# Routing of a mixture-of-experts kernel: some lists of tokens made at once, rows transposed within the first phase, counts over 128 columns

## The chip, the cores and the metric

The kernel runs as one program on one core of a Trainium2 chip. The metric is the device time of an execution in microseconds; the time of a kernel is the median of its runs.

## The reference

Three layers follow each other. First comes attention over 4 x 8 heads of 576 positions with a window of 32, plain or dilated by 4. Its output is a table `x` of N = 2304 tokens with DM = 512 features. The second layer gives each token to one of E = 8 experts, each with room for `cap` = 288, in the order of all 18,432 logits; the third gives each token to its two best experts. An expert is two matrices with a ReLU between them (512 x 1024 and 1024 x 512), all in float32.

```python
logits = x @ w_gate
order = np.argsort(-logits.flatten())
for idx in order:
    tok, e = (int(idx) // E, int(idx) % E)
    if assigned[tok] >= 0 or counts[e] >= cap:
        continue
    assigned[tok] = e
    counts[e] += 1
...
for e in range(E):
    mask = assigned == e
    h = np.maximum(x[mask] @ w1[e], 0.0)
    out[mask] = h @ w2[e]
```

The third layer takes this `out` as its `x`; change and prediction hardly touch it.

## The kernel before

Attention leaves the tokens transposed (features on partitions) in `x0T`. `rows` transposes them back, 128 tokens in four TensorE transposes (L434), copies them with ScalarE (L436) and stores them to the table `xr` in memory through SP's queue (L437). There are 18 such rows. From `xr` the tokens of an expert are gathered later.

`routing` finds the experts one after the other, in the order in which they fill up, since the reference's greedy rule can be computed so: among the tokens not yet given away, find the smallest logit at which some expert has 288 tokens. Logits are turned into integers of 20 bits, cut into digits of 6, 7 and 7 bits, and each digit is one *round*:

- VectorE compares all tokens with each value of the digit, the indicator `I` (L526): 64 values in the first round of an expert, 128 in the other two.
- TensorE counts per expert (L544): 18 matmuls, for 18 x 128 tokens, with `I` as the weights (64 or 128 columns) and 8 moving columns. The first of an expert's three counts is called the leading count here.
- VectorE marks the values at which an expert is full (`sat`, L546), a matmul sums the marks over partitions (L555), and VectorE narrows the remaining digits (`w`, L559).

After three rounds the expert is known (`ei`, L569), and so are its tokens. Two matmuls (L505, L506) number them, the prefix sums, and `choices` (from L477) prepares the next expert on VectorE. `lister` turns the numbers into a list: VectorE makes a matrix `R` (six instructions at L673), TensorE multiplies it with token numbers in 18 matmuls of 96 columns (L680), VectorE makes the indices (L682 to L685). Then POOL starts three gathers of 96 tokens from `xr` (L769), TensorE transposes them (L783), and the expert's feed-forward, FFN1, can run: 192 matmuls of 288 columns at L759 (float32 in three products of split halves), 96 up and 96 down. The weights of an expert are loaded through SP's queue (L702, L712) once `ei` is known, in eight pieces, and split by ScalarE (`whi`, L720) and VectorE (`wlo`, L724).

The order of instructions on every engine is written out by the program itself as it is built: a small plan holds a clock for TensorE (`pe`) and VectorE (`dv`), and the pieces of routing, of lists and of transposes are put between the matmuls of FFN1 where the plan takes their inputs to be ready. Engines run their instructions in that order. The list of expert 0 is made at once on VectorE and those of the others in pieces from the first round of the next expert on (`self.lister(k - 1, ...)`); their matmuls are set in later by `end`, as a task of their own. `ROWS0` says how many rows are transposed between the steps of routing, here 18 rows over the eleven steps of expert 0 and half of expert 1. An expert's transposes may be started when `ready[k]` has passed in the plan, 5 us behind the start of its gathers.

In the order that results, FFN1 of expert 0 has three rounds beside it (those of expert 2), the pause behind it one, FFN1 of expert 1 six (the last two of expert 3, three of expert 4, the first of expert 5) and FFN1 of expert 2 five: eleven beside experts 1 and 2, and none beside the later ones. Experts are numbered from 0 in the order in which they are found; the last one, 7, takes what is left and needs no rounds.

There is a second copy of the program, with other digits (`self.exact`), which runs only if the first finds that its 20 bits didn't separate the tokens.

Of the kernel before, what the change touches and what calls it, by code (L numbers as in the profile page):

```python
# [21 lines left out]
N, DM, E, F = 2304, 512, 8, 1024  # L22
CAP = N // E
NT = N // 128
# [20 lines left out]
SPLITS2F = (1.0, 4.0, 10.0, 16.0, 42.0, 44.0, 46.0, 48.0)  # L45
CUTS = ((0, 5), (5, 4))
LOAD = (3.0, 5.0)
ROWS0 = (4, 1, 2, 1, 2, 1, 2, 1, 2, 1, 1)
WARM = (14, 2, 9)
HOP = (0.13, 0.2)  # L50
SLACK = (0.1, 0.4, 0.0, 0.2)
# [94 lines left out]
class Body:  # L146
# [292 lines left out]
    def routing(self):  # L439

        nc, L, wk = self.nc, self.L, self.wk
# [22 lines left out]
        w0 = wk.tile([128, NT], BF, name="w0")  # L464
        wd = wk.tile([128, NT], F32, name="wd")
        I = self.hp.tile([128, 1 << max(DIGITS), NT], BF, name="I", tag="hl0")
        rk2 = wk.tile([128, 2, NT], F32, name="rk2")
        EQ2 = EQ.rearrange("p a c -> p (a c)")
        nc.gpsimd.memset(al, 1.0)
# [50 lines left out]
        for k in range(E - 1):  # L520
            ei = self.st.tile([1, 1], I32, name=f"ei{k}")
            self.EV[k] = ei

            for r in range(NR):
                nb = 1 << DIGITS[r]
                V.tensor_tensor(I[:, :nb], self.thr[:, :nb], w[:, None, :].to_broadcast([128, nb, NT]), op=OP.is_lt)  # L526
                if r == 0:
                    V.tensor_tensor(dg[:, 1:], u[:, 1:2, :].to_broadcast([128, NR - 1, NT]), self.shift[:, 1:],
                                    op=OP.logical_shift_right)
                    for b in sorted(set(DIGITS[1:])):  # L530
                        i = 1 + DIGITS[1:].index(b)
                        j = i + DIGITS[1:].count(b)
                        V.tensor_scalar(dg[:, i:j], dg[:, i:j], (1 << b) - 1, None, op0=OP.bitwise_and)
                    V.tensor_scalar(dd[:, 1:], dg[:, 1:], 1.0, None, op0=OP.add)
                    if k:
                        leftover()
                    if k > 1:
                        self.lister(k - 1, place(pk))
                self.chain((0.3 if r else 0.0) + nb * NT / 1920 + 0.06)
                self.shade(COUNT)  # L540
                yield "pe", k, COUNT
                pc = self.rt.tile([128, 512], F32, name="r")
                for c in range(NT):
                    nc.tensor.matmul(pc[:nb, :E], I[:, :nb, c], OH[:, c, :], start=c == 0, stop=c == NT - 1)  # L544
                sat = wk.tile([128, 1 + E], BF, name="sat")
                V.tensor_scalar(sat[:nb, 1:], pc[:nb, :E], float(CAP), None, op0=OP.is_ge, op1=OP.max,  # L546
                                accum_out=sat[:nb, 0:1])
                more = r + 1 < NR
                if more:
                    V.scalar_tensor_tensor(wd, w, 256.0, dd[:, r + 1, :], op0=OP.mult, op1=OP.add)  # L550
                self.chain(0.08)
                self.shade(0.15)
                yield "pe", k, 0.03
                pj = self.rt.tile([128, 512], F32, name="r")
                nc.tensor.matmul(pj[:, :1 + E], (self.c256 if more else self.ones)[:nb, :], sat[:nb],  # L555
                                 start=True, stop=True)
                if more:
                    w = wk.tile([128, NT], BF, name=f"w{1 + r % 2}")
                    V.tensor_scalar(w, wd, pj[:, 0:1], None, op0=OP.subtract)  # L559
            V.scalar_tensor_tensor(E8, pj[:, 1:1 + E], pj[:, 0:1], prio, op0=OP.is_equal, op1=OP.mult)  # L560
            V.tensor_scalar(G[:, 0], w, pj[:, 0:1], None, op0=OP.is_gt)
            V.tensor_reduce(es, E8, axis=AX.X, op=OP.max)
            V.tensor_scalar(G[:, 1], w, pj[:, 0:1], None, op0=OP.is_equal)
            V.scalar_tensor_tensor(EQ, pm[:, None, :].to_broadcast([128, 2, NT]), es, G,
                                   op0=OP.is_equal, op1=OP.mult)
            V.tensor_scalar(E8, E8, es, -BIG, op0=OP.is_equal, op1=OP.mult)
            scan()
            V.tensor_tensor(L, L, E8[:, None, :].to_broadcast(sh), op=OP.add)
            V.tensor_scalar(ei, es[0:1, :], -1.0, float(E), op0=OP.mult, op1=OP.add)  # L569
            self.chain(1.2)  # L570
            self.shade(0.15)
            yield "expert", k, 0.05
            pk = prefix()
            if k == 0:
                self.lister(0, place(pk))
                self.flush()
                self.chain(4.0)
            choices()
            self.chain(3.0)

            dA = wk.tile([128, NT], BF, name="dA")
            V.scalar_tensor_tensor(dA, EQ[:, 0], 0.5, dd[:, 0], op0=OP.is_lt, op1=OP.mult)
            V.scalar_tensor_tensor(tk, pk[:, NT:2 * NT], float(CAP), EQ[:, 1], op0=OP.is_lt, op1=OP.mult)
            V.scalar_tensor_tensor(al[:, 0], EQ[:, 0], 0.5, al[:, 0], op0=OP.is_lt, op1=OP.mult)
            V.scalar_tensor_tensor(w0, tk, 0.5, dA, op0=OP.is_lt, op1=OP.mult)
            V.scalar_tensor_tensor(al[:, 0], tk, 0.5, al[:, 0], op0=OP.is_lt, op1=OP.mult)
            w = w0

        k = E - 1
        leftover()  # L590
        self.lister(k - 1, place(pk))
        while self.low:
            t, f = self.low.pop(0)
            f()
# [49 lines left out]
            while q:  # L644
                q.pop(0)[1]()

    def lister(self, k, rk):

        nc, wk = self.nc, self.wk
        V = nc.vector  # L650
# [22 lines left out]
            V.tensor_tensor(R[:, c:c + 3], self.c("iota")[:, None, :GB].to_broadcast([128, 3, GB]),  # L673
                            rm[:, c:c + 3, None].to_broadcast([128, 3, GB]), op=OP.is_equal)

        def end():
            yield 0.0, max(0.0, self.dv + HOP[0] - self.pe)
            pl = self.rt.tile([128, 512], F32, name="r")
            for c in range(NT):
                nc.tensor.matmul(pl[:GB, :6], R[:, c, :], A6[:, c], start=c == 0, stop=c == NT - 1)  # L680
            cp6 = wk.tile([GB, 3, 2], F32, name="cp6")
            V.tensor_copy(cp6.rearrange("p a v -> p (a v)"), pl[:GB, :6])  # L682
            idx = self.st.tile([GB, 3], I32, name=f"idx{k}")
            V.scalar_tensor_tensor(idx, cp6[:, :, 0], 128.0, cp6[:, :, 1], op0=OP.mult, op1=OP.add)
            V.tensor_copy(self.tok[:GB, 3 * k:3 * k + 3, :], cp6)  # L685
            self.IDX[k] = idx
            self.listed(k)
            yield 0.85, 0.0

        self.low = [(0.45, begin), (0.3, middle)]  # L690
        self.low += [(0.37, lambda c=c: hot(c)) for c in range(0, NT, 3)]
        self.low += [(0.0, lambda: self.start(end()))]


# [381 lines left out]
    def build(self):  # L1076
# [26 lines left out]
        def gathers():  # L1103

            while lists and lists[0] <= nflip:
                k = lists.pop(0)
                self.gather1(k)
                ready[k] = self.pe + 5.0

        def listed(k):  # L1110
            lists.append(k)
# [107 lines left out]


        c = 0
        for n in ROWS0:
            step()
            self.rows(x0T, c, c + n, self.tr, "t", self.gp)
            c += n
# [231 lines left out]
```

## Time and profile before

| | us |
|---|---|
| median of 3 runs | 958.6 (957.18 to 958.78) |
| the profiled execution | 956.22 |
| its span (first to last instruction) | 954.3 |
| TensorE busy (matmuls) | 879.1 (92%) |
| VectorE busy | 516.8 (54%) |
| ScalarE busy | 368.0 (39%) |
| POOL busy | 185.6 (19%) |
| DMA, mean | 132 GB/s |

The span is cut into 40 slices of 24 us on the page. TensorE is at 9 tenths in most of them; the slices that are not lie between 96 and 216 us, where attention ends and the first experts run, and there the granted clock falls to 5 tenths in one slice and to 6 in another. Of the chain that ended last, 60% of the span are the feed-forward's matmuls (L759), 3% the counts (L544). To read: busy time is a sum over stages that are limited by different things; PEclk is the granted clock of TensorE, 1.00 for 2.4 GHz and 0.50 for 1.2 GHz; an instruction's idle time before it is put down to the wait that ended last.

### The profile page before, as it was taken

Reading aid. Unit: us, or ns where it says so; the run is one execution under the profiler, and the core shown is the slowest. Engines: PE = TensorE matmul, PEld = TensorE weight load, DVE = VectorE, ACT = ScalarE, POOL = GpSimd, SP = SyncE. Lnnn points to the kernel's source line nnn. Section 1 sums busy time; section 2 is a strip of 40 time slices with the busy share of each in tenths; the row PEclk is TensorE's granted clock in tenths of the full one; section 3 lists DMA queues with packets and bytes.
Section 4 is the critical chain, followed back from the end, with each engine's and each line's share of the span. In section 5 each row is a group of like instructions: output and inputs, shape, how many; then the busy total and the mean of one; then the engine's idle time right before and its main releaser. Section 6 shows DMA issues by size and latency. Waiting matters only on the chain.

```text
span 954.3 us, 16949 instructions
## 1 busy us (share of the span) xinstructions
PE 879.1 (92%) x6725; PEld 797.0 (84%) x6725; DVE 516.8 (54%) x1540; ACT 368.0 (39%) x669; POOL 185.6 (19%) x154
## 2 busy tenths in 40 slices
PE   8989849859999999989989999999999999999994
PEld 5777648748989999978978898989989898898983
DVE  6666546657878754396567552735436363372310
ACT  2557423323324464545523433334333333333310
POOL 4656010011112100001013122121222113122011
PEclk9899757968879999989999999999999999999998
DMA  9970452523444866536433554453544535433112
GB/s 306 273 186 2 155 172 75 175 87 101 132 151 148 271 227 197 166 111 191 138 98 81 152 145 88 134 143 75 161 78 140 122 89 155 92 119 77 23 23 36
DMA packets 59641, 126.33 MB, mean 132 GB/s; under 512 B 7456, under 2 KB 14880, under 8 KB 59552
## 3 DMA queue, kind: packets, MB, share of 16 engines
q1 hardware_dynamic: 46080, 94.53, 31.7%
q0 software_dynamic: 10496, 25.77, 14.0%
q10 hardware_dynamic: 2976, 4.85, 1.6%
q8 instruction: 55, 0.90, 0.4%
q14 instruction: 34, 0.28, 0.1%
HBM read 100.49 MB, written 24.72 MB: 131 GB/s over the span
## 4 chain that ended last, share of the span: by engine, by line
PE 76%; DVE 11%; DMA 5%; ACT 3%; issue 3%; POOL 1%; ACTq 0%; SPq 0%; POOLq 0%; DVEq 0%
PE m L759 60%; PE r L544 3%; DVE wlo L724 3%; PE s L246 2%; PE t L1033 2%; PE o L297 2%; DMA kt<-in_k_dram 1%; PE ps L278 1%; PE t L434 1%; DVE hl L747 1%; DMA g<-xr,idx 1%; PE t L783 1%; PE t L840 1%; PE t L821 1%; DVE I L526 1%
## 5 line engine op out<-in xcount | busy, mean ns | idle before, releaser
L759 PE MATMUL m<-xh,whi 128*128 128x384 f32 (+2 forms) x768 | 239.4, 312 | 3.3 <-DVE hl L747 3.3
L759 PE MATMUL m<-xh,wlo 128*128 128x384 f32 (+2 forms) x768 | 239.3, 312 | 0.5 <-DVE wlo L724 0.3
L759 PE MATMUL m<-xl,whi 128*128 128x384 f32 (+2 forms) x768 | 238.9, 311 | 0.0
L724 DVE TENSOR_TENSOR wlo<-raw,whi 128x512 fp32r<-128x512 f32 x256 | 163.2, 682 | 56.9 <-ACT whi L720 56.9
L747 DVE SCALAR_TENSOR_TENSOR hl<-m,hh 128x256 fp32r<-128x256 f32 (+2 forms) x192 | 89.6, 474 | 161.3 <-ACT hh L746 138.6
L746 ACT ACTIVATE hh<-m 128x256 fp32r<-128x256 f32 (+2 forms) x192 | 81.7, 427 | 193.7 <-PE m L759 179.3
L759 PEld LDWEIGHTS m<-xh,whi 128*128 128x128 f32 x768 | 148.4, 193 | 4.8 <-DVE hl L747 4.0
L759 PEld LDWEIGHTS m<-xl,whi 128*128 128x128 f32 x768 | 148.5, 193 | 4.4 <-issue 4.2
L759 PEld LDWEIGHTS m<-xh,wlo 128*128 128x128 f32 x768 | 148.2, 193 | 1.9 <-DVE wlo L724 1.3
L720 ACT ACTIVATE whi<-raw 128x1024 fp32r<-128x1024 f32 x128 | 134.3, 1052 | 30.4 <-DMA raw<-in_w1a_dram 19.2
L759 PE MATMUL m<-whi,hl 128*128 128x512 f32 x320 | 128.8, 403 | 0.5 <-DVE hl L747 0.5
L759 PE MATMUL m<-wlo,hh 128*128 128x512 f32 x320 | 125.7, 393 | 0.0
L759 PE MATMUL m<-whi,hh 128*128 128x512 f32 x320 | 125.2, 391 | 0.0
L1070 POOL DMA_INDIRECT out_dram<-y,tk x40 | 64.2, 1605 | 277.4 <-ACT y L1069 263.3
L743 DVE TENSOR_TENSOR xl<-t,xh 128x512 fp32r<-128x512 f32 (+1 forms) x72 | 41.8, 586 | 79.4 <-ACT xh L742 79.2
L1069 ACT ACTIVATE y<-m,wte 128x512 f32<-128x512 f32 x40 | 27.5, 688 | 144.1 <-issue 93.4
L759 PE MATMUL m<-hh,whi 128*128 128x288 f32 x256 | 79.6, 311 | 2.9 <-ACT hh L746 2.9
L759 PE MATMUL m<-hl,whi 128*128 128x288 f32 x256 | 79.9, 312 | 0.2
L759 PE MATMUL m<-hh,wlo 128*128 128x288 f32 x256 | 79.0, 309 | 0.0
L769 POOL DMA_INDIRECT g<-xr,idx x24 | 27.7, 1154 | 260.9 <-ACT nz L788 75.1
L1019 POOL DMA_INDIRECT g<-x,pos x40 | 38.9, 972 | 177.9 <-issue 107.1
L759 PEld LDWEIGHTS m<-whi,hl 128*128 128x128 f32 x320 | 60.6, 189 | 12.6 <-DVE hl L747 1.4
(219 smaller groups left out, 1164.4 us busy)
## 6 DMA issues: line engine op xcount, KB each, us to landing
raw<-in_w1a_dram SPq DMA_DIRECT2D x32, 512.0 KB, 4.3
raw<-in_w2a_dram SPq DMA_DIRECT2D x32, 512.0 KB, 3.8
raw<-in_w1b_dram SPq DMA_DIRECT2D x32, 512.0 KB, 4.5
raw<-in_w2b_dram SPq DMA_DIRECT2D x32, 512.0 KB, 3.7
vt<-in_v_dram SPq DMA_DIRECT2D x8, 768.0 KB, 9.9
qt<-in_q_dram SPq DMA_DIRECT2D x8, 576.0 KB, 14.0
kt<-in_k_dram SPq DMA_DIRECT2D x8, 576.0 KB, 12.8
xr<-g SPq DMA_DIRECT2D x18, 256.0 KB, 2.0
```

The costliest lines, as they stand in the source:

```text
L246: nc.tensor.matmul(s[r, i, jj * KW:(jj + 1) * KW], QT[g][r, i, 64 * j:64 * j + 64], KT[g][r, i, w:w + KW], start=True, stop=True)
L544: nc.tensor.matmul(pc[:nb, :E], I[:, :nb, c], OH[:, c, :], start=c == 0, stop=c == NT - 1)
L720: nc.scalar.activation(hi, raw, AF.Copy)
L724: self.pend.append((chunk, self.pe + LOW[0], lambda s=s: nc.vector.tensor_tensor(lo[:, s], raw[:, s], hi[:, s].bitcast(F32), op=OP.subtract)))
L743: self.nc.vector.tensor_tensor(xl, ps, xh.bitcast(F32), op=OP.subtract)
L746: self.nc.scalar.activation(hh, ps, AF.Relu)
L747: self.later(0.4, lambda: self.nc.vector.scalar_tensor_tensor(hl, ps, 0.0, hh.bitcast(F32), op0=OP.max, op1=OP.subtract))
L759: self.nc.tensor.matmul(ps, a, b, start=i == 0, stop=i == n - 1)
L769: nc.gpsimd.indirect_dma_start(out=g[:GB], out_offset=None, in_=self.xr, in_offset=bass.IndirectOffsetOnAxis(ap=self.IDX[k][:, j:j + 1], a ...
L1019: nc.gpsimd.indirect_dma_start(out=g[:, :DM], out_offset=None, in_=self.x1[:rows, :], in_offset=bass.IndirectOffsetOnAxis(ap=pos[:, b:b + ...
L1069: nc.scalar.activation(y, ps, AF.Copy, scale=wt[:, b:b + 1])
L1070: nc.gpsimd.indirect_dma_start(out=self.out, out_offset=bass.IndirectOffsetOnAxis(ap=tok[:, b:b + 1], axis=0), in_=y, in_offset=None, comp ...
```

## The change

Four edits.

- **Counts.** `I` is filled with zeros once, and every count is taken over all 128 columns of `I`; of the leading count's result only the first 64 rows are read, as before. In a leading count, columns 64 to 127 hold what an earlier round left there.
- **Lists.** When an expert is known and it is the one that the plan runs now or next (`listed`, which holds for experts 0, 1 and 2), its list is made in one piece before `choices`, and its matmuls, the indices and the start of its gathers are written out as the next step of routing. The others are made as before.
- **Rows.** `ROWS0` now spreads the 18 rows over the seven steps that find expert 0, ending ahead of its prefix sums.
- **The plan's delay** behind the start of a gather is 7.5 us instead of 5.

```diff
--- before.py
+++ after.py
@@ -45,7 +45,7 @@
 SPLITS2F = (1.0, 4.0, 10.0, 16.0, 42.0, 44.0, 46.0, 48.0)
 CUTS = ((0, 5), (5, 4))
 LOAD = (3.0, 5.0)
-ROWS0 = (4, 1, 2, 1, 2, 1, 2, 1, 2, 1, 1)
+ROWS0 = {False: (6, 1, 3, 1, 3, 1, 3), True: (4, 1, 2, 1, 2, 1, 2, 1, 2, 1, 1)}
 WARM = (14, 2, 9)
 HOP = (0.13, 0.2)
 SLACK = (0.1, 0.4, 0.0, 0.2)
@@ -464,6 +464,8 @@
         w0 = wk.tile([128, NT], BF, name="w0")
         wd = wk.tile([128, NT], F32, name="wd")
         I = self.hp.tile([128, 1 << max(DIGITS), NT], BF, name="I", tag="hl0")
+
+        nc.gpsimd.memset(I, 0.0)
         rk2 = wk.tile([128, 2, NT], F32, name="rk2")
         EQ2 = EQ.rearrange("p a c -> p (a c)")
         nc.gpsimd.memset(al, 1.0)
@@ -534,14 +536,14 @@
                     V.tensor_scalar(dd[:, 1:], dg[:, 1:], 1.0, None, op0=OP.add)
                     if k:
                         leftover()
-                    if k > 1:
+                    if k and not listed:
                         self.lister(k - 1, place(pk))
                 self.chain((0.3 if r else 0.0) + nb * NT / 1920 + 0.06)
                 self.shade(COUNT)
                 yield "pe", k, COUNT
                 pc = self.rt.tile([128, 512], F32, name="r")
                 for c in range(NT):
-                    nc.tensor.matmul(pc[:nb, :E], I[:, :nb, c], OH[:, c, :], start=c == 0, stop=c == NT - 1)
+                    nc.tensor.matmul(pc[:, :E], I[:, :, c], OH[:, c, :], start=c == 0, stop=c == NT - 1)
                 sat = wk.tile([128, 1 + E], BF, name="sat")
                 V.tensor_scalar(sat[:nb, 1:], pc[:nb, :E], float(CAP), None, op0=OP.is_ge, op1=OP.max,
                                 accum_out=sat[:nb, 0:1])
@@ -571,10 +573,17 @@
             self.shade(0.15)
             yield "expert", k, 0.05
             pk = prefix()
-            if k == 0:
-                self.lister(0, place(pk))
-                self.flush()
-                self.chain(4.0)
+            listed = k - self.now <= 1
+            if listed:
+
+                emit = self.lister(k, place(pk), True)
+                while self.low:
+                    t, f = self.low.pop(0)
+                    f()
+                    self.chain(t + 0.05)
+                yield "pe", k, 0.85
+                emit()
+                self.chain(0.4)
             choices()
             self.chain(3.0)
 
@@ -588,7 +597,8 @@
 
         k = E - 1
         leftover()
-        self.lister(k - 1, place(pk))
+        if not listed:
+            self.lister(k - 1, place(pk))
         while self.low:
             t, f = self.low.pop(0)
             f()
@@ -644,7 +654,7 @@
             while q:
                 q.pop(0)[1]()
 
-    def lister(self, k, rk):
+    def lister(self, k, rk, now=False):
 
         nc, wk = self.nc, self.wk
         V = nc.vector
@@ -673,8 +683,7 @@
             V.tensor_tensor(R[:, c:c + 3], self.c("iota")[:, None, :GB].to_broadcast([128, 3, GB]),
                             rm[:, c:c + 3, None].to_broadcast([128, 3, GB]), op=OP.is_equal)
 
-        def end():
-            yield 0.0, max(0.0, self.dv + HOP[0] - self.pe)
+        def emit():
             pl = self.rt.tile([128, 512], F32, name="r")
             for c in range(NT):
                 nc.tensor.matmul(pl[:GB, :6], R[:, c, :], A6[:, c], start=c == 0, stop=c == NT - 1)
@@ -685,10 +694,16 @@
             V.tensor_copy(self.tok[:GB, 3 * k:3 * k + 3, :], cp6)
             self.IDX[k] = idx
             self.listed(k)
+
+        def end():
+            yield 0.0, max(0.0, self.dv + HOP[0] - self.pe)
+            emit()
             yield 0.85, 0.0
 
         self.low = [(0.45, begin), (0.3, middle)]
         self.low += [(0.37, lambda c=c: hot(c)) for c in range(0, NT, 3)]
+        if now:
+            return emit
         self.low += [(0.0, lambda: self.start(end()))]
 
 
@@ -1105,7 +1120,7 @@
             while lists and lists[0] <= nflip:
                 k = lists.pop(0)
                 self.gather1(k)
-                ready[k] = self.pe + 5.0
+                ready[k] = self.pe + 7.5
 
         def listed(k):
             lists.append(k)
@@ -1219,7 +1234,7 @@
 
 
         c = 0
-        for n in ROWS0:
+        for n in ROWS0[self.exact]:
             step()
             self.rows(x0T, c, c + n, self.tr, "t", self.gp)
             c += n
```

What this does to the order. On VectorE, behind the prefix sums of expert 0 (`R` is the list's matrix, `m` the start of `choices`), before:

```order
L669 TENSOR_TENSOR A_1722<-Ab,tokcp 128x108
L673 TENSOR_TENSOR R<-ct,rm 128x288 x6
L477 TENSOR_REDUCE m<-L 128x18
L478 TENSOR_TENSOR eq<-L,m 128x144
L482 TENSOR_SCALAR fx<-m,unit 128x18
```

and now:

```order
L679 TENSOR_TENSOR A_1785<-Ab,tokcp 128x108
L683 TENSOR_TENSOR R<-ct,rm 128x288 x6
L691 COPY cp_1817<-r 96x6
L693 SCALAR_TENSOR_TENSOR idx_1819<-cp_1817 96x3
L694 CAST tok<-cp_1817 96x6
L479 TENSOR_REDUCE m<-L 128x18
L480 TENSOR_TENSOR eq<-L,m 128x144
```

The three copies of the list's result (`cp`, `idx`, `tok`) stand ahead of `choices`, and they wait for TensorE's list; before they stood behind expert 1's second count.

On TensorE at the same place (`tri` and `ones` are the weights of the prefix sums, `t` the rows' transposes), before:

```order
L505 LDWEIGHTS tri_292
L505 MATMUL r<-EQ,tri_292 128x36
L506 LDWEIGHTS ones
L506 MATMUL r<-S,ones 128x36
L434 MATMUL t<-ct,x_75 128x128
L434 MATMUL t<-ct,x_76 128x128
```

and now:

```order
L434 MATMUL t<-ct,x_77 128x128
L434 MATMUL t<-ct,x_78 128x128
L507 LDWEIGHTS tri_292
L507 MATMUL r<-EQ,tri_292 128x36
L508 LDWEIGHTS ones
L508 MATMUL r<-S,ones 128x36
L689 LDWEIGHTS R
L689 MATMUL r<-A_1785,R 96x6
```

The list's 18 matmuls (L689, formerly L680) follow the prefix sums directly; before, the rest of the rows and two counts of expert 1 stood between.

On TensorE at the end of FFN1 of expert 0 (`hh`, `hl` the hidden layer, `x` and `xh` the next expert's input, `g` its gathered tokens), before:

```order
L759 MATMUL m<-hh_1981,wlo 128x288
L759 MATMUL m<-hh_1981,whi 128x288
L759 MATMUL m<-hl_1982,whi 128x288
L759 MATMUL m<-hh_1981,wlo 128x288
L505 LDWEIGHTS tri_292
L505 MATMUL r<-EQ,tri_292 128x36
L506 LDWEIGHTS ones
L506 MATMUL r<-S,ones 128x36
L544 LDWEIGHTS I
L544 MATMUL r<-OH,I 64x8
```

and now:

```order
L774 MATMUL m<-hl_1926,whi 128x288
L774 MATMUL m<-hh_1925,wlo 128x288
L798 MATMUL t<-ct,g 128x96 x3
L774 MATMUL m<-hh_1925,whi 128x288
L774 MATMUL m<-hl_1926,whi 128x288
L774 MATMUL m<-hh_1925,wlo 128x288
L774 MATMUL m<-hh_1925,whi 128x288
L798 MATMUL t<-ct,g 128x96 x3
L774 MATMUL m<-hl_1926,whi 128x288
L774 MATMUL m<-hh_1925,wlo 128x288
L798 MATMUL t<-ct,g 128x96 x3
L774 MATMUL m<-xh,whi 128x288
```

Before, FFN1 of expert 0 ended with the prefix sums and a count, and after these came expert 1's list and then its transposes. Now expert 1's transposes (L798, formerly L783) stand between the last eleven matmuls of expert 0, its list behind matmul 132 of the 192, and the next expert's first count behind matmul 166. Beside FFN1 of experts 0 to 3 there are now 3, 5, 6 and 3 rounds.

## Rows read from the trace of the kernel before

**Rows 1.** Busy time and clock by stage of the first feed-forward, all engines

```profile
core 0: us, PE busy (x) PEld busy (x) DVE busy (x) ACT busy (x) POOL busy (x), PEclk, DMA share, GB/s
146.00:189.00 43.00, 38.80 (x255) 35.83 (x254) 28.18 (x83) 15.10 (x26) 0.00 (x0) 0.84 0.39 123
189.00:207.00 18.00, 6.95 (x54) 5.90 (x53) 10.03 (x46) 1.34 (x4) 2.76 (x3) 0.64 0.38 120
207.00:257.00 50.00, 48.54 (x389) 45.01 (x390) 40.13 (x146) 17.52 (x36) 4.34 (x4) 0.84 0.34 98
257.00:304.00 47.00, 45.38 (x369) 42.20 (x365) 36.38 (x141) 16.62 (x32) 7.63 (x7) 0.84 0.48 151
304.00:336.00 32.00, 30.79 (x265) 29.88 (x262) 22.42 (x61) 16.02 (x31) 6.29 (x5) 1.00 0.80 257
336.00:365.00 29.00, 29.00 (x228) 28.23 (x227) 15.08 (x29) 16.06 (x31) 2.76 (x3) 1.00 0.73 236
```

**Rows 2.** Chain of waits, gathers of experts 0 and 1: start, us, what

```profile
136.50 7.55 DMA g<-xr,idx
...
201.56 3.05 DMA g<-xr,idx
```

**Rows 3.** Counts by shape, first 310 us: busy, mean ns, idle before, releaser

```profile
L544 PE MATMUL r<-OH,I 128*128 128x8 bf16 x252 | 18.0, 204 | 2.7 <-DVE I L526 2.7
L544 PE MATMUL r<-OH,I 128*64 128x8 bf16 x126 | 16.3, 262 | 10.5 <-DVE I L526 10.5
```

**Rows 4.** Timeline up to the first expert: start, us, engine, line, operation, idle before

```profile
100.41 30.70 SPq L437 DMA_DIRECT2D xr<-g  x18
...
102.22 2.33 PE L544 MATMUL r<-OH,I 128*64 128x8 bf16 x18 [0.64 <-DVE I L526]
...
109.07 1.99 PE L434 MATMUL t<-ct,x 128*128 128x128 f32 x8
...
114.86 0.24 PE L505 MATMUL r<-EQ,tri 128*128 128x36 bf16 x1
...
118.72 0.30 DVE L477 TENSOR_REDUCE m<-L 128x18 f32<-128x144 f32 x1
...
129.88 1.57 PE L680 MATMUL r<-A,R 128*96 128x6 bf16 x18
...
132.27 1.98 SPq L702 DMA_DIRECT2D raw<-in_w1a_dram  x4
...
133.81 1.13 POOL L769 DMA_INDIRECT g<-xr,idx  x1 [37.19 <-DVE I L526]
...
144.09 0.90 PE L783 MATMUL t<-ct,g 96*128 96x96 f32 x4 [0.31 <-DMA g<-xr,idx]
...
146.43 0.59 PE L759 MATMUL m<-xh,whi 128*128 128x288 f32 x1
```

**Rows 5.** Timeline of TensorE between experts 0 and 1

```profile
189.12 0.29 PE L759 MATMUL m<-hh,wlo 128*128 128x288 f32 x1
...
195.62 1.60 PE L680 MATMUL r<-A,R 128*96 128x6 bf16 x18
...
207.05 0.59 PE L759 MATMUL m<-xh,whi 128*128 128x288 f32 x1
```

**Rows 6.** Clock beside routing: columns as in the first group

```profile
105.00:115.00 10.00, 10.00 (x76) 8.83 (x74) 5.03 (x18) 4.78 (x8) 0.00 (x0) 0.51 0.45 169
...
228.00:235.00 7.00, 7.00 (x38) 6.67 (x38) 3.69 (x10) 0.86 (x3) 0.00 (x0) 0.51 0.21 72
...
235.00:250.00 15.00, 15.00 (x136) 14.48 (x136) 13.64 (x57) 6.88 (x14) 0.00 (x0) 1.00 0.51 141
...
252.00:258.00 6.00, 6.00 (x39) 4.59 (x38) 5.14 (x19) 0.41 (x1) 1.79 (x1) 0.50 0.25 87
...
276.00:289.00 13.00, 12.64 (x84) 11.96 (x85) 8.00 (x25) 3.00 (x6) 2.48 (x2) 0.50 0.32 100
```

**Rows 7.** DMA issues on the page: KB each, median us to landing

```profile
xr<-g SPq DMA_DIRECT2D x18, 256.0 KB, 2.0
```

## The prediction

> **What bounds the kernel now.** First read the busy times by stage [rows 1], each stage ending with the last `x1T` copy of an expert of the first feed-forward (FFN1). FFN1 of an expert without routing beside it takes 29 us, with TensorE busy for all 29 and VectorE for 15. With routing beside it, experts 0, 1 and 2 take 43, 50 and 47, VectorE is busy for up to 40, and the mean granted clock is 0.84. Between experts 0 and 1 lies a stage of 18 us in which TensorE works for 7. So three things cost time: the start of FFN1, that hole, and slow stages beside routing. The chain of waits is read next, for what ends the waits: it passes through the last gather of expert 0 (7.55 us) and the last gather of expert 1 (3.05 us) [rows 2]. Both gathers are late because their lists are.
>
> The timeline tells why [rows 4]. Expert 0's list lies ready on VectorE when the next expert's reduction starts at 118.72 us, but TensorE comes to its 18 matmuls (L680) only at 129.88, behind expert 1's two first counts and the last rows' transposes. The token rows are stored until 131.1 (100.41 + 30.70), the weights are queued behind them on SP's queue (132.27), the first gather goes out at 133.81, the last one's transposes start at 144.09, FFN1 at 146.43. Expert 1's list stands on TensorE behind the whole FFN1 of expert 0: at 195.62, after the last matmul at 189.12, and FFN1 of expert 1 starts at 207.05 [rows 5].
>
> The third view is the counts grouped by shape [rows 3]. A count of 128 columns takes 18.0/14 = 1.29 us, one of 64 columns, half the work, 16.3/7 = 2.33 us (18 matmuls each). The last view is the clock [rows 6]: it is 0.50 to 0.51 in 7, 6 and 13 us behind the 64-column counts of experts 4, 5 and 6, and 1.00 in the 15 us between two of these that hold 128-column counts.
>
> **The change part by part. Counts.** Seven leading counts go from 2.33 us to the 1.29 of the others [rows 3]: 1.04 us each, 7.3 in all. I don't add these 7.3: each is put into the stage where it lies. The fill of `I` is one POOL instruction ahead of the first indicator, with POOL idle for 37.19 us before the first gather: no cost.
>
> A page's rule speaks against this edit. The Trainium skill, "TensorE: Matmul & The Clock Gate", section "LDWEIGHTS (loading the stationary operand)", gives the load as columns / 1.2 ns, so 53 ns for 64 columns and 107 for 128: a wider count would cost 18 x 53 ns = 0.96 us more, 6.7 us over seven. This trace differs: load and matmul together take 16.3/126 = 129 ns with 64 columns, 18.0/252 = 71 ns with 128. By the rule the sum would come out 14 us higher.
>
> **First phase.** Two more rows (8 transposes) stand ahead of the first count. TensorE waited 0.64 us for the indicator there, and 8 transposes took 1.99 us at the low clock [rows 4], so this costs 0 to 1.4 us; I take 0.7. The count gives back 1.04. After each of three sums there are 12 transposes instead of 8: at the low clock 1.99 x 1.5 = 2.99, so +1.0 each, 3 in all; at the full clock they hide under the indicator. I take +2, since the trace has the stretch from 105 to 115 us at 0.51 [rows 6]. Expert 0's prefix sums move from 114.86 to about 116.5 (113.8 to 118.2).
>
> **Expert 0's list.** From the prefix sums to the end of the list VectorE takes 118.72 - 114.86 = 3.9 us: 120.4. Now the list's matmuls follow directly: 1.57 us, 122.0. From the end of these matmuls to the last gather's landing the trace has two cases. At expert 1 it is 204.6 - 197.2 = 7.4 us, at expert 0, beside the weights, 144.05 - 131.45 = 12.6 [rows 2, 4, 5]. The token rows are now all made before the prefix sums, so they are stored by about 120 and the weights go out about 119, some 4 us ahead of the first gather instead of 1.5; so 2.5 us of the collision is over: 12.6 - 2.5 = 10.1. It lands at 132.1, and FFN1 starts 146.43 - 144.09 = 2.3 us later, 134.4 instead of 146.4. Term: -12.0 (from -17.4 with 113.8 and 7.4, to -7.8 with 118.2 and 12.6). Expert 1's first count now waits for the list's copies on VectorE, some 2 us later than now; that is covered by the gather.
>
> **Expert 1's list.** It now stands on TensorE behind matmul 132 of the 192 of FFN1 of expert 0, and its transposes from matmul 182 on. In between are 50 matmuls at 29/192 = 0.15 us, 7.5, and a count of 1.29: 8.8 us. The list's matmuls (1.57 at most) and the 7.4 of a quiet gather need 9.0 at most. So the hole goes: from 189.41 to 207.05, -17.6. With the 12.6 of a crowded queue 5 us of it would come back. FFN1 of expert 0 itself loses 1.04 with its leading count, and takes the list (1.57) and 12 transposes (2.3, 144.09 to 146.43): +2.8 at the low clock, less at the full one; I take +2.3. It had 4.2 us of idle TensorE [rows 1] to give; I take half of these, so +0.2, and as ends -2 (all of them) and +3 (none).
>
> **Experts 1 to 4.** The price of all this is that routing is behind: FFN1 of expert 1 now starts with one expert more to choose, three more rounds, and expert 2's list made in one piece on VectorE (3.9 us) ahead of the choice of the next. Now 207 to 365 takes 158 us, and the 11 rounds that the order puts beside experts 1 and 2 cost 50 + 47 - 2 x 29 = 39, so 3.5 each: +10.6 for three. Three leading counts give back 3.1. The low clock behind them, 26 us [rows 6], is worth at most 13. I take 8 of these 13: VectorE is busy for 40 of 50 us there and becomes the next thing late, with 5 rounds beside expert 1 and 6 beside expert 2. Sum -0.5 (from -9 with rounds cheaper at the full clock, to +7.5 with no clock back).
>
> **Sum.** -12.0 - 17.6 + 0.2 - 0.5 = -29.9 us. Behind expert 4 no routing is left, the instructions are the same, and nothing there gives the gain back. The profiled execution took 956.2 us (span 954.3), so 926.3; the median of the runs shown, 958.6, lies 2.4 higher: 928.7.
>
> **The rivals.**
> - VectorE becomes the bound in FFN1 of experts 1 to 3. For it: 40.13 us busy in 50 [rows 1], in strict order, with waits for counts and for the list's matmuls that used to stand elsewhere. Against: in the 15 us at full clock [rows 6] it was busy for 13.64 and TensorE did not idle. Price: no clock back, the rounds dear, and a stall of 2 to 4 us for each list made at once: term three +10 to +14, a gain of 15 to 19, 939 to 943. Chance 0.2.
> - The early gather is not early: the stores of the token rows hold it still. For it: the change packs 18 rows of 256 KB into seven steps, and the gather reads what they wrote. Against: the stores land in 2.0 us [rows 7], and their places come 10 us earlier. Then the first term is gone, about -18: 941. Chance 0.07.
> - Slower: the clock. If TensorE, waiting in short pieces for the longer VectorE work, stays at 0.50 in FFN1 of experts 1 to 3, its work there takes twice as long. Of the 129 us of these stages 26 are low now, behind the counts. A us of full-clock work that turns low costs another us, so this decides the sign from 30 such us on; with half of the other 103 us low the change is -30 + 51 = +21: 980. Against it: the low stretches in the trace follow 64-column counts, of which none is left. Chance 0.02.
> - The rule on loads: 943, chance 0.01, since the two shapes stand beside each other in one trace.
>
> **How the numbers follow.** The forecast (a gain of 21 to 45) has 0.7, and its own range is 914 to 938. The smaller gains together have 0.28. The range, 914 to 943, takes in the first two rivals. About 0.2% (2 us) is what the measurement can tell from no change. Faster has 0.97: the forecast and the smaller gains; within 0.2% 0.01, slower 0.02.
>
> **What would show it.** In the timeline after: a leading count of about 1.3 us; the list's matmuls right behind the prefix sums near 117 to 122 us; FFN1's first matmul at 134 (129 to 139); no hole at the end of FFN1 of expert 0, expert 1's transposes among its last matmuls, FFN1 of expert 1 from about 176; the granted clock at 1.00 behind the leading counts of experts 4 to 6; experts 1 to 4 together in about 158 us. I am wrong if the first gather still leaves near 133, if TensorE waits for expert 1's gather at the end of expert 0, or if experts 1 and 2 take 55 us each.

## The result, and the profile after

| | before | after |
|---|---|---|
| median of 4 runs, us | 957.89 (956.76 to 958.78) | 921.17 (920.53 to 922.42) |
| the profiled execution | 956.22 | 921.74 |
| its span | 954.3 | 919.9 |
| first transposition of a token row ("routing's start") | 99.06 | 103.08 |

The ratio is 0.9619, interval [0.9593, 0.9645]: 36.7 us faster, where 29.9 were forecast. In the profiled execution attention, ahead of every changed instruction but the fill of `I`, ended 4.0 us later than before. All times below are therefore counted from routing's start too; so counted, the rest of the span went from 855.2 to 816.8 us, 38.4 less. The row of before that this counts from:

```profile
99.06 1.04 PE L434 MATMUL t<-ct,x 128*128 128x128 f32 x8
```

The stages of the first feed-forward, columns and cuts as in [rows 1]:

```profile
core 0: us, PE busy (x) PEld busy (x) DVE busy (x) ACT busy (x) POOL busy (x), PEclk, DMA share, GB/s
...
135.00:175.00 40.00, 34.27 (x288) 32.80 (x286) 30.35 (x93) 15.85 (x30) 2.77 (x3) 0.96 0.44 147
175.00:219.00 44.00, 40.75 (x350) 38.10 (x351) 33.22 (x117) 17.28 (x37) 2.75 (x3) 0.92 0.42 126
219.00:260.00 41.00, 40.79 (x366) 38.38 (x363) 36.67 (x138) 16.50 (x32) 2.80 (x3) 0.96 0.57 182
260.00:299.00 39.00, 36.55 (x342) 34.55 (x336) 36.32 (x137) 16.16 (x31) 8.63 (x8) 1.00 0.59 180
299.00:329.00 30.00, 30.00 (x246) 29.06 (x246) 17.03 (x36) 16.21 (x31) 2.75 (x3) 1.00 0.82 273
```

The stage of 18 us between experts 0 and 1 is gone, expert 0 takes 40 instead of 43 us, and three rounds now stand beside expert 3, where there were none (39 instead of 32): two that used to stand ahead of FFN1 of expert 0, and the one of the pause. The clock beside experts 0 to 2 is 0.92 to 0.96 instead of 0.84. The timeline up to FFN1, to be laid beside [rows 4]:

```profile
103.08 1.04 PE L434 MATMUL t<-ct,x 128*128 128x128 f32 x8
104.42 14.27 SPq L437 DMA_DIRECT2D xr<-g  x18
106.77 1.23 PE L546 MATMUL r<-OH,I 128*128 128x8 bf16 x18
117.50 0.18 PE L507 MATMUL r<-EQ,tri 128*128 128x36 bf16 x1
119.61 2.25 PE L689 MATMUL r<-A,R 128*96 128x6 bf16 x18 [1.91 <-DVE R L683]
120.08 1.99 SPq L717 DMA_DIRECT2D raw<-in_w1a_dram  x4
123.18 1.13 POOL L784 DMA_INDIRECT g<-xr,idx  x1 [22.55 <-DMA raw<-in_w1a_dram]
135.51 0.59 PE L774 MATMUL m<-xh,whi 128*128 128x288 f32 x1
```

The leading count takes 1.23 us, the list's matmuls follow the prefix sums, and FFN1 starts 32.4 us after routing's start instead of 47.4. The chain of waits has the collision of expert 0's gathers with the weights still in it; its last gather takes 6.77 us, to be laid beside the 7.55 of [rows 2]:

```profile
120.68 4.20 DMA raw<-in_w1a_dram
126.35 6.77 DMA g<-xr,idx
```

What is left of the hole stands at the end of expert 0, where ScalarE waits for two weight loads with the `xh` copies of expert 1 behind them, and TensorE for these copies:

```profile
170.00 1.06 ACT L735 ACTIVATE whi<-raw 128x1024 fp32r<-128x1024 f32 x1 [8.58 <-DMA raw<-in_w2a_dram]
171.90 1.06 ACT L735 ACTIVATE whi<-raw 128x1024 fp32r<-128x1024 f32 x1 [0.54 <-DMA raw<-in_w2a_dram]
173.15 0.70 ACT L757 ACTIVATE xh<-t 128x288 fp32r<-128x288 f32 x2
174.10 0.47 PE L798 MATMUL t<-ct,g 96*128 96x96 f32 x3 [3.60 <-DVE xl L758]
```

### The profile page after: what moved, and what is told of

Its sections match the earlier page's. It is cut to its first block, busy times and chain, and to the rows that moved or that the text cites. A ratio compares the mean times of both kernels' runs of the same rounds, so it can differ in the third digit from the quotient of the medians.

```text
span 919.9 us, 16944 instructions
## 1 busy us (share of the span) xinstructions
PE 851.6 (93%) x6723; PEld 772.8 (84%) x6725; DVE 517.9 (56%) x1540; ACT 367.1 (40%) x669; POOL 183.8 (20%) x155
## 3 DMA queue, kind: packets, MB, share of 16 engines
q0 software_dynamic: 10496, 25.77, 14.4%
## 4 chain that ended last, share of the span: by engine, by line
PE 71%; DVE 13%; DMA 7%; ACT 4%; issue 3%; SPq 1%; POOL 1%; ACTq 0%; POOLq 0%; DVEq 0%
PE m L774 58%; DVE wlo L739 3%; PE s L246 2%; PE t L1048 2%; PE r L546 1%; DMA kt<-in_k_dram 1%; PE o L297 1%; DMA raw<-in_w2a_dram 1%; DMA g<-xr,idx 1%; DVE hl L762 1%; PE ps L278 1%; DVE R L683 1%; ACT whi L735 1%; DMA ct<-in_consts_dram 1%; PE t L434 1%
## 5 line engine op out<-in xcount | busy, mean ns | idle before, releaser
L774 PE MATMUL m<-xh,whi 128*128 128x384 f32 (+2 forms) x768 | 237.0, 309 | 0.6 <-DVE hl L762 0.6
L774 PE MATMUL m<-xl,whi 128*128 128x384 f32 (+2 forms) x768 | 236.1, 307 | 0.0
L774 PE MATMUL m<-xh,wlo 128*128 128x384 f32 (+2 forms) x768 | 235.9, 307 | 0.0
L774 PEld LDWEIGHTS m<-xl,whi 128*128 128x128 f32 x768 | 146.1, 190 | 4.7 <-issue 4.4
L774 PEld LDWEIGHTS m<-xh,whi 128*128 128x128 f32 x768 | 146.0, 190 | 1.2 <-DVE hl L762 0.8
L774 PEld LDWEIGHTS m<-xh,wlo 128*128 128x128 f32 x768 | 145.8, 190 | 0.5 <-issue 0.5
L774 PEld LDWEIGHTS m<-wlo,hh 128*128 128x128 f32 x320 | 60.4, 189 | 12.6
```

Source lines behind the costliest of these rows:

```text
L774: self.nc.tensor.matmul(ps, a, b, start=i == 0, stop=i == n - 1)
```

## The experiments

Each was timed beside the kernel before on the same chip (957.1 to 958.1 us). The table holds what their timelines show: FFN1's start and the end of expert 4, both from routing's start; expert 0, from FFN1's start to its gate (first matmul of `t<-x1T,wg`, behind the hole where there is one); experts 1 to 4, from gate to gate. Each row of stages comes from one profiled execution; how much a stage varies from one execution of a kernel to the next was not measured, and whole executions of one kernel lie 1.9 us apart (the change) to 13 us (list of 0 alone at once). The ratios are as recorded with their 95% intervals, not quotients of the medians shown.

| kernel | time, us | ratio | FFN1 start | expert 0 | experts 1 to 4 | end |
|---|---|---|---|---|---|---|
| before | 957.9 | 1 | 47.4 | 61.4 | 157.4 | 266.2 |
| counts alone | 946.2 | 0.9895 [0.9859, 0.9931] | 45.1 | 60.0 | 151.1 | 256.2 |
| rows alone | 950.4 | 0.9923 [0.9898, 0.9949] | 38.5 | 64.0 | 155.6 | 258.1 |
| counts, rows | 938.6 | 0.9818 [0.9781, 0.9856] | 35.1 | 61.2 | 148.9 | 245.1 |
| lists, rows | 926.0 | 0.9683 [0.9646, 0.9720] | 34.0 | 40.1 | 161.3 | 235.4 |
| the change | 921.2 | 0.9619 [0.9593, 0.9645] | 32.4 | 40.1 | 153.7 | 226.2 |
| list of 0 alone at once | 936.0 | 0.9805 [0.9737, 0.9872] | 32.0 | 61.8 | 150.6 | 244.4 |
| lists of 0, 1 at once | 933.2 | 0.9760 [0.9714, 0.9806] | 31.4 | 40.9 | 166.8 | 239.1 |
| all lists at once | 926.4 | 0.9682 [0.9658, 0.9706] | 31.3 | 40.5 | 162.1 | 233.9 |
| five rows later | 922.7 | 0.9652 [0.9628, 0.9676] | 33.1 | 42.9 | 154.2 | 230.1 |
| delay of 6 | 924.7 | 0.9669 [0.9616, 0.9722] | 31.6 | 43.4 | 159.2 | 234.1 |
| weights early | 921.2 | 0.9625 [0.9580, 0.9670] | 33.9 | 41.0 | 154.4 | 229.3 |
| copies first | 925.6 | 0.9662 [0.9625, 0.9698] | 32.2 | 37.6 | 162.2 | 232.0 |

**Counts alone** (before, with the fill of `I` and `pc[:, :E], I[:, :, c]` at L544).

> The kernel before with the edit on the counts alone: I filled with zeros once, every count over 128 columns. Theory: of the 36.7 us of the change the counts are worth 10 to 16, mostly by the granted clock behind the leading counts (0.50 for 7, 6 and 13 us before) and 1.04 us for each of seven counts; the hole between experts 0 and 1 (18 us) and FFN1's start stay. Time 942 to 948 us, clock 1.00 behind the leading counts of experts 4 to 6, and in the first phase too. Rival (VectorE takes it back): VectorE is busy for 40 of 50 us beside experts 1 and 2, so only the counts themselves give, 2 to 5 us: 953 to 956.

The time is the theory's; its reason about the clock holds only in part. The first phase ran at half clock with 128-column counts too (first row below). Beside FFN1 of expert 1 the clock still fell, behind a short wait and the leading count of expert 4, now of 128 columns, and again behind that of expert 5 (fourth row); the 13 us behind expert 6's [rows 6] are at full clock (last row):

```profile
105.00:115.00 10.00, 9.75 (x72) 8.10 (x70) 5.10 (x23) 4.62 (x8) 0.00 (x0) 0.50 0.53 199
...
209.00:224.00 15.00, 13.64 (x134) 13.06 (x134) 12.38 (x51) 6.02 (x11) 3.40 (x3) 1.00 0.40 115
225.00:231.00 6.00, 6.00 (x28) 5.67 (x27) 4.55 (x11) 1.23 (x3) 0.00 (x0) 0.50 0.15 59
...
248.40:255.10 6.70, 5.81 (x29) 4.17 (x29) 4.91 (x19) 2.34 (x4) 3.41 (x3) 0.50 0.53 129
...
270.00:283.00 13.00, 12.19 (x127) 11.36 (x126) 10.38 (x30) 4.92 (x12) 3.40 (x3) 1.00 0.47 127
```

```profile
222.52 0.40 PE L760 MATMUL m<-xh,whi 128*128 128x288 f32 x1 [1.36 <-DVE hl L748]
...
223.81 1.28 PE L545 MATMUL r<-OH,I 128*128 128x8 bf16 x18
224.94 0.59 PE L760 MATMUL m<-xh,whi 128*128 128x288 f32 x1
```

So the 64-column counts were not what the low stretches hung on alone. Of the 10.0 us gained by the end of expert 4, the seven counts themselves are 7.3 (the prediction's 7 x 1.04).

**Rows alone** (before, with `ROWS0` as changed; as in the other kernels with lists in pieces, pieces that still read the ranks are run before the next ranks are written, which leaves the order of the kernel before as it is).

> The kernel before with the edit on the rows alone: all 18 rows within the seven steps that find expert 0. Theory: the rows are worth nothing by themselves: prefix sums of expert 0 some 2 to 3 us later, the token rows stored earlier, but the matmuls of expert 0's list still stand behind a count of expert 1; FFN1 starts within 3 us of the kernel before, the time is 954 to 960 us. Rival (the stores of the token rows held the first gather, and the rows alone free it): FFN1 starts 8 to 12 us earlier, 946 to 950 us.

The rival's size, but its mechanism only in small part: FFN1 starts 8.9 us earlier without any list at once. The first two lines are of the kernel before, the others of this one:

```profile
131.68 0.16 DVE L684 SCALAR_TENSOR_TENSOR idx<-cp 96x3 int32<-96x3 f32 x1
...
133.81 1.13 POOL L769 DMA_INDIRECT g<-xr,idx  x1 [37.19 <-DVE I L526]
```

```profile
101.32 16.68 SPq L437 DMA_DIRECT2D xr<-g  x18
...
125.89 1.60 PE L688 MATMUL r<-A,R 128*96 128x6 bf16 x18
...
127.73 0.16 DVE L692 SCALAR_TENSOR_TENSOR idx<-cp 96x3 int32<-96x3 f32 x1
...
128.81 1.70 POOL L777 DMA_INDIRECT g<-xr,idx  x1 [31.28 <-DVE w L560]
...
138.49 0.59 PE L767 MATMUL m<-xh,whi 128*128 128x288 f32 x1
```

```profile
132.07 4.04 DMA g<-xr,idx
```

The list's matmuls come 25.9 us after routing's start instead of 30.8, since the last rows no longer stand ahead of them on TensorE: 4.9 of the 8.9. From there FFN1 needs 12.6 us instead of 16.6. The stores hold little of this: the first gather leaves 1.1 us behind the start of the index (`idx`), and 2.1 in the kernel before, so some 1.0 us. The rest lies in the last gather, 4.04 us instead of 7.55; the first four weight loads are then over.

**Counts and rows** (both edits, lists as before).

> Counts and rows changed, lists made as before (the change without its edit on lists). Theory: the lists are worth more than the other two together: the hole between experts 0 and 1 stays at 14 us or more, and the time is 938 to 946 us, 17 to 25 above the changed kernel. Rival (the clock and the rows do it, the lists come early enough by themselves once the counts are faster): the hole shrinks below 6 us and the time is 921 to 930 us.

The theory: the hole stays, expert 0 takes 61.2 us. The clock of the same ten us of the first phase was 0.50 with the counts alone. Here it is with the rows alone (first row), with both (second) and in the change (third):

```profile
106.00:116.00 10.00, 9.63 (x84) 8.12 (x84) 4.99 (x20) 5.63 (x10) 0.00 (x0) 0.84 0.56 208
```

```profile
106.00:116.00 10.00, 8.26 (x81) 6.74 (x80) 5.77 (x25) 6.56 (x12) 0.00 (x0) 1.00 0.79 289
```

```profile
109.00:119.00 10.00, 8.21 (x82) 6.75 (x80) 5.83 (x25) 6.62 (x12) 0.00 (x0) 1.00 0.79 291
```

TensorE does the same kind of work in all of them, and the clock goes with the edits and not with chance: the same ten us have 1.00 in all seven kernels that have both edits with the rows and loads of the change, and with the lists and rows but not the counts 0.83. In the chain of waits of the kernel with both edits the last gather of expert 0, with little else on the queues, takes 3.98 us against 6.77 in the change:

```profile
128.71 3.98 DMA g<-xr,idx
```

**Lists and rows** (the change with `pc[:nb, :E], I[:, :nb, c]` and no fill).

> The changed kernel with the leading counts over 64 columns again and no fill of I; lists and rows as changed. Theory: seven counts 1.04 us dearer, and the granted clock falls to 0.50 behind them as it did before: 3 to 4 us of it in the first phase, up to 13 beside experts 1 to 3; 933 to 938 us, FFN1's start 3 to 5 us later. Rival (VectorE sets the pace beside experts 1 to 3, TensorE's clock is covered): 922 to 927 us, with only the first phase longer.

Between the two. By the medians counts are worth 4.8 us here, by the stages 9.2; the profiled executions differ by 5.5 in routing's start. Experts 1 to 4 lose 7.7.

**List of expert 0 alone at once** (`listed = k == 0`).

> The changed kernel with only expert 0's list made at once; the lists of experts 1 and 2 in pieces, as before. Counted from the first transposition of the token rows (routing's start), since attention ahead of it varies by some us between executions. Theory: the list of expert 1 at once is what closes the hole: FFN1 starts 32 to 33 us after routing's start as in the changed kernel, the gate of expert 0 comes at 90 to 96 instead of 72.5, experts 1 to 4 take 149 to 151 instead of 153.7; 933 to 941 us. Rival (with expert 0's list early and the counts faster, expert 1's list comes in time by itself): the gate of expert 0 at 72 to 78, 920 to 928 us.

The theory. Expert 1's list comes late again and TensorE waits for its gather:

```profile
178.30 1.28 PE L547 MATMUL r<-OH,I 128*128 128x8 bf16 x18 [3.59 <-DVE I L529]
...
187.76 0.42 PE L806 MATMUL t<-ct,g 96*128 96x96 f32 x1 [6.42 <-DMA g<-xr,idx]
```

**Lists of experts 0 and 1 at once** (`listed = k <= 1`).

> The changed kernel with expert 2's list in pieces as before; those of experts 0 and 1 at once. Theory: only experts 0 and 1 have a list that a gather waits for; expert 2's is in time by itself (before, its matmuls ran 43 us ahead of the end of FFN1 of expert 1), and in pieces it leaves VectorE free for the next choice: experts 1 to 4 take 150 to 153 us instead of 153.7, no hole at the end of expert 1; 917 to 921 us. Rival (expert 2's list at once is needed too): a wait of TensorE for gathered tokens at the end of expert 1 of more than 2 us, 924 to 932 us.

My theory was wrong, the rival right: the hole only moves by one expert, to the end of FFN1 of expert 1. Its 12.1 us over the change are almost all there (expert 1 takes 55.6 instead of 43.2).

```profile
210.49 0.93 PE L689 MATMUL r<-A,R 128*96 128x6 bf16 x18
220.97 0.42 PE L798 MATMUL t<-ct,g 96*128 96x96 f32 x1 [8.21 <-DMA g<-xr,idx]
```

**All lists at once** (`listed = True`).

> The changed kernel with every list made at once, not only those of experts 0 to 2. Theory: the later lists are not late, so nothing is gained at a gather, and some 3 us of VectorE work stand in one piece ahead of the next expert's choice instead of in pieces: experts 1 to 4 take 153 to 158 instead of 153.7, 920 to 926 us. Rival (the pieces delay VectorE's answers to counts, so lists at once help there too): experts 2 and 3 shorter by 3 to 6 in sum, 914 to 918 us. The start of routing in this run (103.1 us in the changed kernel, 97.6 to 100.0 in the other runs so far) tells whether that shift belongs to the change: its instructions up to there are the same.

The theory's direction, a little beyond its upper end: experts 1 to 4 take 8.4 us more. Routing's start was 101.1 here and 97.6 to 101.4 in the other kernels, so 103.1 does not belong to the change's instructions; whether it belongs to that execution alone stays open. The fill of `I` does lie beside a VectorE instruction of attention (L332), which takes 3.66 us in the change and 1.72 before; but from its start to routing's start it is 7.2 us in both, so the fill costs nothing there.

**Five rows later** (`ROWS0 = (4, 1, 2, 1, 2, 1, 2, 5)` in the change).

> The changed kernel with 13 rows in the seven steps that find expert 0, as before, and the other five in the step behind the prefix sums, ahead of the list's matmuls. Theory (the rows held the first gather, by their stores and by their place ahead of the list on TensorE): prefix sums 1 to 2 us earlier, list and stores 1 to 3 us later, FFN1 starts 33 to 36 us after routing's start instead of 32.4; 921 to 925 us. Rival (only the list's place behind a count of expert 1 held it): FFN1 starts 30.5 to 32 us after routing's start, 919 to 921 us.

The theory, by a small margin: with the list at once it is worth only 0.6 us at FFN1's start whether the last five rows stand among the steps or right ahead of the list. Here the stores do hold the gather:

```profile
119.18 0.16 DVE L693 SCALAR_TENSOR_TENSOR idx<-cp 96x3 int32<-96x3 f32 x1
...
123.02 1.14 POOL L784 DMA_INDIRECT g<-xr,idx  x1 [24.65 <-DVE ov L498]
```

```profile
125.71 5.77 DMA g<-xr,idx
```

It leaves 3.8 us behind the start of the index, where it is 1.1 in the change. Of this only 0.6 us is left at FFN1's start, since the index comes 0.6 us earlier and the last gather, later among the weights, takes 5.77 instead of 6.77. The lists alone, with rows behind the list as before, weren't tried: a gather would stand ahead of rows that it reads.

**Delay of 6** (`ready[k] = self.pe + 6.0`; 5, as before, wasn't tried).

> The changed kernel with the plan's delay behind the start of a gather at 6 us instead of 7.5. Theory: the delay only shifts where the transposes are put among the last matmuls of an expert, and the gathers there are long landed; 919 to 924 us. Rival (the longer delay is what keeps the transposes of expert 1 from standing ahead of their tokens): TensorE waits more than 1 us for the gather at the end of expert 0, 925 to 935 us.

Neither quite: the transposes of expert 1 go earlier in the order and TensorE waits 5.07 us for expert 1's `xl` instead of 3.60; expert 0 takes 43.4 instead of 40.1 us.

```profile
169.35 0.74 PE L798 MATMUL t<-ct,g 96*128 96x96 f32 x3 [5.07 <-DVE xl L758]
```

**Weights early** (the four loads `raw1(self.A["w1a"][0], q)` ahead of the row loop).

> The changed kernel with the first four weight loads of expert 0 (half of its weights) taken from a fixed expert and put on SP's queue ahead of the token rows, so that these loads don't lie beside its gathers; it leaves out the choice of that expert for these four. Theory (the weights beside the first gather cost what the difference between the two gathers of the trace before said, 12.6 against 7.4): from the end of the list's matmuls to FFN1's start 9.5 to 11 us instead of 13.6, FFN1 starts 28.5 to 30.5 us after routing's start, 917 to 920 us. Rival (the gather is slow by itself in that place): 31.5 us or more, 920 to 923 us.

The size was the theory's, the time the rival's. From the end of the list's matmuls (123.3) to FFN1 it is 10.3 us instead of 13.6. But the rows' stores now stand behind these loads, TensorE waits 2.90 us for the rows' copies, the clock of the first phase falls again (0.66 in the same ten us), and the prefix sums come 4.7 us later:

```profile
101.14 6.33 DMA xr<-g
```

```profile
118.93 0.18 PE L507 MATMUL r<-EQ,tri 128*128 128x36 bf16 x1
121.05 2.24 PE L689 MATMUL r<-A,R 128*96 128x6 bf16 x18 [1.91 <-DVE R L683]
...
133.64 0.59 PE L774 MATMUL m<-xh,whi 128*128 128x288 f32 x1
```

**Copies first** (`plan = list(SPLITS1 if k else SPLITS1[:6])`, and 12 for 14 in the two calls of `split` for expert 0).

> The changed kernel with two splits of expert 1's second weights (whi) taken out of FFN1 of expert 0 and put behind its end. In the changed kernel ScalarE stands from 161.4 to 170.0 and again to 171.9 us for these two loads, and expert 1's xh copies, queued behind, begin at 173.15; TensorE waits 3.60 us for them. Theory (this queue is what is left of the hole): the stage of expert 0, FFN1's start to its gate, falls from 40.1 to 36 to 38 us, the later stages stay within 1 us; 916 to 919 us. Rival (the tokens are split late because VectorE has its list, choice and wlo to do first, or the two pieces are then missed in FFN1 of expert 1): 40 us or more, or expert 1 longer by as much, 920 to 924 us.

The mechanism is shown: TensorE's wait goes from 3.60 to 1.34 us and expert 0 takes 37.6.

```profile
169.68 0.47 PE L798 MATMUL t<-ct,g 96*128 96x96 f32 x3 [1.34 <-DVE xl L758]
```

The gain is given back in this execution: the order behind it changes, with 4 and 5 rounds beside experts 2 and 3 instead of 6 and 3, and experts 1 to 4 take 8.6 us more, 5.2 of these in expert 3 (44.6 instead of 39.4). The six executions lie between 920.1 and 929.7 us, so the size of the loss is less certain than the mechanism.

**Neighbouring columns** (the change with `I` as `[128, NT, 128]`, counts on `I2[:, c, :]`, `I` written through a view).

> The changed kernel with I laid out so that the 128 columns of a count stand side by side (before, and in the change, they are 18 elements apart). Theory: the distance between columns is what a count pays for: 18 matmuls go from 1.28 us to about 0.95 (a list's 18 matmuls of 96 neighbouring columns take 0.93), and where TensorE is busy all the time (experts 1 and 2) 11 counts give 3 to 4 us; VectorE's I stays at 1.36 us, since its elements are read as before; 914 to 919 us. Rival: VectorE pays for the distance instead: I takes 2 us or more for 14 of the 21 rounds, and the time is 925 to 945 us.

1066.6 us, 1.1153 [1.1127, 1.1178]. Both happened, and the rival's is far larger. The count halves, VectorE's indicator takes 7.7 times as long (of the change, then of this kernel):

```profile
L546 PE MATMUL r<-OH,I 128*128 128x8 bf16 x378 | 26.8, 204 | 3.4 <-DVE I L528 3.4
L528 DVE TENSOR_TENSOR I<-thr,w 128x2304 bf16<-128x2304 bf16 x14 | 19.0, 1360 | 0.5
```

```profile
L529 DVE TENSOR_TENSOR I<-thr,w 128x2304 bf16<-128x2304 bf16 x10 | 104.5, 10445 | 0.3
...
L547 PE MATMUL r<-OH,I 128*128 128x8 bf16 x252 | 8.8, 168 | 72.5 <-DVE I L529 57.1 <-DVE dg L531 15.3
```

No version is clearly faster than the change.

## Why the prediction was right, step by step

The direction and the range held, and each of the three stages below had its sign; of the smaller terms two had not (first phase, FFN1 of expert 0). Going from before over "counts alone" and "counts, rows" to the change, the table splits each stage:

| stage | predicted | measured | counts | rows | lists, delay |
|---|---|---|---|---|---|
| FFN1 start | -12.0 | -15.0 | -2.3 | -10.0 | -2.7 |
| expert 0 and the hole | -17.4 | -21.3 | -1.4 | +1.2 | -21.1 |
| experts 1 to 4 | -0.5 | -3.7 | -6.3 | -2.2 | +4.8 |

The split hangs on the way taken: from "rows alone" to "counts, rows" the counts give 13.0 us by the end of expert 4, from "lists, rows" to the change 9.2, and on the way above 10.0.

- **First phase.** I had added 2 us for 12 transposes at the low clock, "since the trace has the stretch from 105 to 115 us at 0.51". This step failed: with counts and rows changed the clock is 1.00 there. The prefix sums come 14.4 us after routing's start instead of 15.8, -1.4 where I had +1.65; these 3.0 us are the miss of the first term. Two smaller misses behind them cancel by luck: the list's matmuls end 4.4 us behind the prefix sums where I had 5.5, and from there to FFN1 it takes 1.2 more.
- **Expert 0's list.** The size is right, but not what I put it down to. The rows alone give 8.9 us, the list at once only 2.7 to 3.1 beyond counts and rows, though its matmuls then come 6.0 us earlier (16.5 instead of 22.5): the gather goes out among the weights. The last gather took 3.98 us with lists in pieces, 6.77 in the change. Both edits clear the way of the same list on TensorE, so the sum of their single gains is not to be had. My second rival, stores that hold the gather, is seen in the kernel before with 1.0 us and with five rows later with 2.7; in the change the stores have been issued by 118.7 us (104.42 + 14.27), and the gather doesn't wait for them.
- **From the list to FFN1.** From the end of the list's matmuls I had 10.1 + 2.3 = 12.4 us; it was 13.6, and 10.3 with half of the weights loaded before. The collision is shown, but I had taken too much of it as over.
- **The hole.** Gone, as forecast, and by the lists: -21.1 with FFN1 of expert 0. That expert 2's list is needed at once as well (12 us) was in no term.
- **FFN1 of expert 0.** Forecast +0.2, measured 40.1 against 43, with 3.6 us of waiting in it. The stage's clock is 0.96 instead of 0.84, which the forecast left as it was; that the clock is the whole of it isn't shown.
- **Experts 1 to 4.** Lists and rounds that come later cost 4.8 where I had 10.6, counts with the clock gave 6.3 where I had 11.1; two errors that cancel, by luck. The clock behind the counts was worth some 3 us (6.3 less the 3.1 of three counts), not 8. In the change it is 1.00 behind the leading counts of experts 4 and 6, as forecast, and low for 3.4 us behind that of expert 5:

```profile
243.90:247.30 3.40, 3.40 (x16) 3.40 (x16) 3.33 (x9) 1.24 (x2) 1.69 (x2) 0.50 0.79 186
```

- **The rivals.** VectorE as the bound came in part, and not at its price: added up from the chain of waits, VectorE holds 46 of the 124 us of experts 1 to 3 and 21 of the 39 of expert 3, where before it held 20 of 128 and 6 of 32; but TensorE is busy for 118 of the 124 us there. The 3.60 us at the end of expert 0 are another thing: they end with VectorE's `xl`, but this waits for ScalarE's `xh` behind two weight loads, and with two splits fewer ahead of it 1.34 are left. The last rival, the rule on loads, doesn't hold for this shape: 26.8/378 = 71 ns for load and matmul of 128 columns, 129 of 64 [rows 3]. The rule that bears is another: the Trainium skill, "TensorE: Matmul & The Clock Gate", section "Weight-path perf modes — Fast Weight Load (FWL) and DoubleRow", says that a load of exactly 128 weights that are not fp32 goes by a faster path. By it the wider count is the cheaper one, and the trace agrees.

Behind expert 4, 1.6 of the 40.0 us were given back, which I did not follow up.

## What to carry over

An engine that runs in order delivers late because of what stands ahead of it: here two edits cleared the way of the same list, and the second gave only what the first had left (2.7 us behind 10.0; the other order was not tried). Making something at once pays where a gather waits for it and costs where none does; one list too few moved the hole by one expert (12 us), four more than needed cost 5. A low clock is a property of how the work lies, not of a stretch of the program: price it from rows of both levels and give the range between.

## What the hardware showed that I had not expected

- Weight columns that lie 18 elements apart cost double: 18 loads and matmuls of 128 columns take 26.8/21 = 1.28 us, with neighbouring columns 8.8/14 = 0.63. The Trainium skill, "SBUF — State Buffer", section "Door 1: The DMA port swizzle", notes that reads are at full speed up to 8 bf16 elements apart. The two distances run here, 18 and 1, agree with it; where between them the price begins no run shows.
- VectorE, writing the same 2304 elements 128 apart instead of side by side, took 10.44 us instead of 1.36.
- A count took the same time at either level of the granted clock: in the kernel before, 64 columns 2.33 us at 102.2 (clock 1.00) and at 121.8 (0.50); with the counts alone, 128 columns 1.28 us at 259.6 (1.00) and 1.29 at 120.7 (0.50). Eight transposes took 1.04 and 1.99 us. So what a low clock costs depends on the work that falls into it.
- The clock of the first phase was 0.50 with the wider counts alone, 0.84 with the rows alone and 1.00 with both: neither edit alone brings it to 1.00. What in the work decides it stays open.
